# Pieces of q, k and V as closed stretches in memory, and extra rows of a strided V loaded sixteen at a time

## The chip, the cores and the metric

The kernel runs on one core of a Trainium2 chip. The metric is the device time of one execution in microseconds (us); lower is better. Arranging the inputs on the host, before they are copied to the device, is outside it.

## The reference, cut to what matters

Attention over 4 batches and 8 heads of 576 positions with 64 numbers each, then a soft mixture of 8 experts, then a two-layer network with ELU. The first four heads look at the last 32 positions, the other four at every 32nd position ("strided").

```python
B, H, S, D = 4, 8, 576, 64
scores = q @ k^T / sqrt(D)                      # per batch and head
mask_local = (rel >= 0) & (rel < 32)            # heads 0 to 3
mask_strided = (rel >= 0) & (pos_k % 32 == pos_q % 32)   # heads 4 to 7
attn = softmax(where(mask, scores, -1e9)) @ v
x = attn as (2304, 512)
# soft mixture of experts: 8 experts with 4 slots each
logits = x @ phi
slot_in = softmax(logits over tokens).T @ x
slot_out[e] = relu(slot_in[e] @ w1[e]) @ w2[e]  # w1 (8,512,1024), w2 (8,1024,512)
y = softmax(logits over slots) @ slot_out
out = elu(y @ w_in) @ w_out                     # w_in (512,2048), w_out (2048,512)
```

## The kernel before

Heads go in four pairs: p = 0, 1 are the local ones, p = 2, 3 the strided ones. For each pair q, k and V lie in SBUF on all 128 partitions; q and k have QW = 2304 numbers per partition, a strided V has WB = 4096. The host function `_lay` (line 1382) brings the inputs into that order: an array of 128 rows (72 for a strided V) for each pair, whose rows are as long as the whole partition.

The loads are taken in pieces, since attention works through 20 units in a fixed order (`ORDER`, line 39) and the first need only the first columns. `load_q` (line 224) takes columns a to b of 128 rows. `load_k` (line 227) makes two loads, of the even and of the odd rows, each into every second partition. `load_v` (line 234) takes 128 rows for a local V. For a strided V it makes two loads: 64 rows into the even partitions (line 238), and 8 more rows, for the positions from 16 on of a block of 18, into partitions 1, 17, 33, ... 113 (line 239). A strided V has odd partitions that are cleared beforehand: `lv` and line 334 do that on ACT and GpSimd, and the load waits for it. There are four such pairs of loads (two head pairs with two halves of 2048 columns), so a row of such a load is 8 KB. Every one of these loads takes, of each row of its array in memory, only a part: between two rows lie the columns of the other pieces.

All loads are issued by SP's queue, in one order. It comes from `list_order` (line 87), a list scheduler that is run as the program is made, with costs and due times written out by hand; `load_node` (line 457) gives a load's cost by its columns. After the inputs of attention come the experts' matrices, 2 MB each (`load_w`, line 358, issued at line 363), whole or in halves and smaller pieces (`LO`, `HI`), into buffers that attention's tiles leave; such an issue waits for the last reader of the buffer. `emit_w1` (line 919) multiplies the slots with the first matrices, `emit_w2` (line 1009) with the second ones, expert by expert; the matrix of the last expert comes in five pieces (line 967). `warm` (line 308) puts filler matmuls between, at line 313. After the last expert the two-layer network runs (from line 1083), with its own list of operations; its weights are loaded behind the experts' on the same queue (`load_w64`, line 971).

Of the kernel before, what the change touches and what calls it, by code (L numbers as in the profile page):

```python
# [18 lines left out]
@with_exitstack  # L19
def attn_moe_mlp(ctx, tc, q, k, v_l, v_s, phi, w1, w2, w_in, w_out, out):  # L20
    nc = tc.nc
    B, S, D = 4, q.shape[2] // 4, 64
    NT, DM = out.shape
    NE = w1.shape[0]
    w_in, w_out = w_in.bitcast(I32), w_out.bitcast(I32)
# [51 lines left out]
    QW, WB = S * B, 4096  # L77
# [127 lines left out]
    qk_t, v_t = {}, {}  # L205
# [10 lines left out]
    VT = {2: v2_sb, 3: v3_sb, 0: v0_sb[:, 0:QW], 1: v0_sb[:, QW:2 * QW]}  # L216
    for p, q_sb in ((2, q2_sb), (3, q3_sb[:, 0:QW]), (0, q3_sb[:, QW:2 * QW]), (1, q2_sb)):
# [3 lines left out]
        else:  # L221
            v_t[p] = VT[p][:, 0:WB].rearrange("p (t h w r d) -> p t h w r d", t=2, h=2, w=2, d=D)

    def load_q(p, a, b):
        nc.sync.dma_start(out=qk_t[p][0][:, a:b], in_=q[p, :, a:b])

    def load_k(p, a, b, es=((0, "S"), (1, "S"))):
        for e, eng in es:
            x = a % (QW // 2)
            (nc.sync if eng == "S" else nc.scalar).dma_start(  # L230
                out=qk_t[p][1][e:128:2, a // (QW // 2), e, x:x + b - a], in_=k[p, e:128:2, a:b]
            )

    def load_v(p, a, b):
        if p < 2:
            nc.sync.dma_start(out=VT[p][:, a:b], in_=v_l[p, :, a:b])
        else:
            nc.sync.dma_start(out=VT[p][0:128:2, a:b], in_=v_s[p - 2, 0:64, a:b])
            nc.sync.dma_start(out=VT[p][1:128:16, a:b], in_=v_s[p - 2, 64:72, a:b])

    units, cnt_p = [], {0: 0, 1: 0, 2: 0, 3: 0}
    for x in ORDER:
        p = {"L": 0, "S": 2}[x]
# [12 lines left out]
    with tc.manual_schedule():  # L256
        kz = [t.rearrange("p (h e x) -> p h e x", h=2, e=2) for t in kAB]
        A0, Q1, HW_ = 768, 1536, QW // 2
        nc.vector.memset(kz[0][:, 0, 0, 0:A0], 0.0)
        nc.gpsimd.memset(kz[0][:, 0, 1, 0:A0], 0.0)  # L260
        load_q(0, 0, Q1)
        load_k(0, 0, A0, ((1, "S"), (0, "S")))
        load_q(2, 0, HW_)
        make_identity(nc, ident)
        wm2 = misc.tile([128, 1], F32, name="wm2")
# [9 lines left out]
        for b in range(B):  # L275
            lm = lcur[32 * b:32 * b + 32]
            nc.gpsimd.affine_select(
                out=lm, in_=lm, compare_op=ALU.is_ge, fill=0.0, base=0, pattern=[[-1, 32]], channel_multiplier=1,
# [4 lines left out]
            out=lkeep[:, 0], in0=lkeep[:, 1], scalar1=0.0, scalar2=None, op0=ALU.is_equal  # L283
# [8 lines left out]
        for b in range(B):  # L292
# [3 lines left out]
                out=sm_, in_=sm_, compare_op=ALU.is_ge, fill=0.0, base=0, pattern=[[-1, MR]], channel_multiplier=1,  # L296
# [20 lines left out]
        for i, h, e, x in ((1, 0, 1, 0), (0, 0, 0, A0), (0, 0, 1, A0), (0, 1, 0, 0), (0, 1, 1, 0)):  # L317
            nc.scalar.activation(
                out=kz[i][:, h, e, x:HW_], in_=zero.to_broadcast([128, HW_ - x]), func=AF.Copy,
            )  # L320
            if i:
                load_k(2, 0, HW_, ((0, "S"), (1, "S")))
# [74 lines left out]
        def emit_ex(t):  # L397
            dT = late_at[t]
            nc.scalar.activation(
                out=dT, in_=logits[:, 192 * t:192 * t + 192], func=AF.Exp, bias=nm[:, t:t + 1],  # L400
                accum_out=dsum[:, t:t + 1],
            )
            dl[t] = dT

        def emit_dt(t):
            dT = dl[t]
            dl[t] = late_at[3 + t].rearrange("p (i x) -> p i x", x=32)
            nc.vector.transpose(out=dl[t], in_=dT.rearrange("p (i x) -> p i x", x=32))
# [19 lines left out]
        def an(eng, dur, deps, key, fn, alloc=None, instr=0):  # L428
            anodes.append((eng, dur, list(deps), key, fn, alloc, 0.0))
            if instr:  # L430
                count[len(anodes) - 1] = instr
            return len(anodes) - 1
# [24 lines left out]
        def load_node(kind, p, a, b, after=(), pre=None):  # L457
            f = {"q": load_q, "k": load_k, "v": load_v}[kind]
            if pre is not None:
                f = lambda *a: None  # L460
            need = min(users(p, kind, a, b))
            key = T[need] - (14 if kind != "v" else 9)
            dur = 128 * 4 * (b - a) / 1e6 * RATE
            if kind == "v" and p >= 2:
                dur *= 0.63
                after = [("n", y) for (k_, x), y in lv.items() if k_ == p and a <= x < b]
            post.append((key if pre is None else pre, dur, after, lambda: f(p, a, b), (kind, p, a, b)))
# [9 lines left out]
        for p in (2, 3):  # L477
            for x in range(2):
                h = (HW_ * x, HW_ * x + HW_)
# [6 lines left out]
        for x in range(2):  # L486
            h = (HW_ * x, HW_ * x + HW_)
# [334 lines left out]
        for n, (p, t, h) in enumerate(units):  # L822
            make_loads()
            evs[n] = unit_nodes(n)
            if n == max(of[3]):
                rm = an("V", 0.2, lt[4:5] + [y for m in of[2] + of[3] for y in qk[m]], T[n] + 30, lambda: nc.vector.tensor_scalar(
                    out=rmask, in0=e0, scalar1=-1.0, scalar2=-NEG, op0=ALU.add, op1=ALU.mult
# [11 lines left out]
            out=nm3[:, 0:1], in_=logits[:, 0:192], axis=AX.X))  # L839
        m = an("V", 1.3, [m], KT + 1, lambda: emit_m(0))  # L840
        x = an("A", 0.4, [m], KT + 2, lambda: emit_ex(0))
        x = an("V", 0.33, [x], KT + 2.5, lambda: emit_dt(0))
# [6 lines left out]
        x = an("P", 1.6, [x] + xe[0], KT + 3, f_acc0, ("t", r_acc), 24)  # L849

        def f_acc0e():
# [6 lines left out]
            out=nm3[:, 1:2], in_=logits[:, 192:384], axis=AX.X))  # L858
        m = an("P", 0.5, [m, rm], KT + 3.5, lambda: emit_mm(1, False), None, 4)
        m = an("V", 0.2, [m], KT + 4, lambda: emit_nm(1))  # L860
        x = an("A", 0.4, [m], KT + 4.3, lambda: emit_ex(1))
        x = an("V", 0.33, [x], KT + 4.8, lambda: emit_dt(1))
        an("V", 0.3, [lg_last[2]], KT + 4.9, lambda: nc.vector.reduce_max(
            out=nm3[:, 2:3], in_=logits[:, 384:576], axis=AX.X))
# [3 lines left out]
        for t, n in order:  # L868
# [17 lines left out]
            out=acc_sb[0], in0=acc1, scalar=wt[:, 1:2], in1=acc_sb[0], op0=ALU.mult, op1=ALU.add  # L886
# [14 lines left out]
        for x in (slice(0, 256), slice(256, 512)):  # L901
            nc.vector.scalar_tensor_tensor(
                out=acc_sb[1][:, x], in0=acc2[:, x], scalar=wt[:, 2:3], in1=acc_sb[0][:, x], op0=ALU.mult, op1=ALU.add
# [11 lines left out]
        for t in (misc.tile([128, 1024], F32, tag="pst", name="h1T"), small("xt", 768, "h1T_b", 1), ssf[:, 0:256]):  # L915
            nc.gpsimd.memset(t, 0.0)
            t = t.rearrange("p (e c s) -> p e c s", c=8, s=NS)
# [188 lines left out]
        def node(eng, dur, deps, key, fn, alloc=None, at=0.0):  # L1106
            kd, hold = HOLD.get(len(nodes), (0.0, -9.0))
            nodes.append((eng, dur, list(deps), key + kd, fn, alloc, max(at, hold)))
            return len(nodes) - 1
# [226 lines left out]
        for si, gi, s, f0, f1, y, T, parts in ev_n:  # L1336
            k = part_n[si, gi, s]
# [18 lines left out]
            x = node("V" if f0 else "A", 0.6 if f0 else 0.48, deps, key, f_ev, ("ob", rel) if f1 == NF else None)  # L1356
            o_rel[k].append(x)
            last[j] = x
            if f1 == NF:
                rel.append(node("S", 0.73, [x], key, lambda j=j, ob=ob, parts=parts: [nc.sync.dma_start(  # L1360
                    out=out[128 * j:128 * j + 128, x], in_=ob["t"][:, x]
# [20 lines left out]
def _lay(np, q, k, v, moe_phi, **rest):  # L1382
    B, H, S, D = q.shape
    def lay(x):


        l = x[:, 0:4].reshape(B, 2, 2, S // 32, 32, D).transpose(1, 5, 2, 3, 0, 4).reshape(2, 2 * D, B * S)
        s = x[:, 4:8].reshape(B, 2, 2, S // 32, 2, 2, 4, 2, D).transpose(1, 8, 7, 4, 5, 2, 6, 0, 3).reshape(2, 2 * D, B * S)
        return np.concatenate([l, s])

    vl = v[:, 0:4].reshape(B, 2, 2, S // 32, 32, D).transpose(1, 0, 4, 3, 2, 5).reshape(2, 128, 4 * S)

    vs = v[:, 4:8].reshape(B, 2, 2, S // 32, 2, 2, 8, D).transpose(1, 0, 3, 4, 5, 2, 6, 7).reshape(2, B, S // 32, 64 * D)
    vs = np.concatenate([x.reshape(2, -1, 64 * D) for x in (vs[:, :, 0:16], vs[:, :, 16:])], axis=1)
    phi = moe_phi.reshape(4, 128, -1).transpose(1, 0, 2).reshape(128, -1)

    w1, w2 = ((w.reshape(w.shape[0], -1, 128, w.shape[2]).transpose(0, 2, 1, 3).reshape(w.shape[0], 128, -1))
              for w in (rest["moe_w1"], rest["moe_w2"]))
    return dict(rest, q=lay(q), k=lay(k), v_l=vl, v_s=vs, moe_phi=phi, moe_w1=w1, moe_w2=w2)


# [23 lines left out]
```

## Time and profile before

| | us |
|---|---|
| median of 3 runs | 358.25 |
| lowest and highest | 357.84, 360.31 |
| span of the profiled execution, first to last instruction | 356.7 |
| PE busy in it | 338.3 |
| DVE, ACT, GpSimd busy in it | 261.0, 248.8, 57.4 |
| bytes moved by transfers | 69.71 MB, 195 GB/s over the span |

The profiled execution is one run with the hardware profiler on; its times are counted from the first instruction, and its span leaves out what a run has around the first and the last instruction. The rows that matter follow in a section of their own. An engine named with a q (SPq) is its queue of issues. "DMA" on the slices is the mean busy share of the 16 DMA engines.

### The profile page before, as it was taken

To read this page: it belongs to the slowest core of one execution; us is meant where nothing else is said; L and a number is where in the kernel's file an instruction comes from. 1 tells how busy PE (TensorE), PEld (TensorE's weight loads), DVE (VectorE), ACT (ScalarE), POOL (GpSimd) and SP (SyncE) were. 2 spreads that over 40 slices of the span, in tenths; PEclk is the share of its full clock that TensorE was granted. 3 is DMA by queue.
4 is the path that set the end of the run, shared out by engine and by line. 5 is a ranking of instruction groups with operands and counts; after the bars stand their busy time and mean duration, and the time that the engine had idled before them with its cause. 6 is when DMAs were issued, how large, how long until landed. Compare 5 with 4: busy or idle time off the path is not lost.

```text
span 356.7 us, 6955 instructions
## 1 busy us (share of the span) xinstructions
PE 338.3 (95%) x2678; PEld 250.5 (70%) x2678; DVE 261.0 (73%) x574; ACT 248.8 (70%) x488; POOL 57.4 (16%) x106
## 2 busy tenths in 40 slices
PE   5689889999999899999999999999999999999995
PEld 3568776783333257787888788888878888888884
DVE  5999888744605069999999999997755674576741
ACT  9488999983216079999978877767656666666650
POOL 8788534520214000000000000000000000000000
PEclk9899999999999999999999999999999999999998
DMA  7999999999999998650006041000000030032301
GB/s 266 377 378 391 407 416 424 420 410 422 423 428 419 405 403 341 243 228 2 1 0 237 1 153 82 2 0 0 2 0 1 2 119 0 31 118 88 118 2 59
DMA packets 15200, 69.71 MB, mean 195 GB/s; under 512 B 1568, under 2 KB 2080, under 8 KB 12320
## 3 DMA queue, kind: packets, MB, share of 16 engines
q1 hardware_dynamic: 15168, 69.28, 49.2%
q8 instruction: 21, 0.34, 0.4%
q14 instruction: 11, 0.09, 0.1%
HBM read 64.55 MB, written 4.72 MB: 194 GB/s over the span
## 4 chain that ended last, share of the span: by engine, by line
PE 74%; DVE 8%; DMA 8%; ACT 5%; POOL 2%; issue 2%; DVEq 0%; SPq 0%; POOLq 0%; ACTq 0%
PE ops L1312 18%; PE ops L1314 18%; PE ops L1313 18%; DMA q<-in_moe_w_dram 6%; PE hps L1264 5%; PE s_ps L923 3%; ACT bd L657 3%; PE o_ps L670 2%; DVE sc L589 1%; DMA kA<-in_k_dram 1%; PE mps L1153 1%; PE xtps L786 1%; DVE sm L613 1%; POOL bd L659 1%; DVE mx L597 1%
## 5 line engine op out<-in xcount | busy, mean ns | idle before, releaser
L1274 DVE SCALAR_TENSOR_TENSOR g<-hps,g 128x512 f32<-128x512 f32 (+1 forms) x80 | 50.6, 633 | 17.8 <-ACT g L1271 17.1
L1268 ACT ACTIVATE g<-hps 128x512 f32<-128x512 f32 (+1 forms) x80 | 44.8, 559 | 13.6 <-PE hps L1264 12.2
L1271 ACT ACTIVATE g<-g 128x512 f32<-128x512 f32 (+1 forms) x80 | 47.6, 595 | 1.5
L1280 ACT ACTIVATE ghi<-g 128x512 fp32r<-128x512 f32 (+1 forms) x40 | 23.7, 592 | 18.3 <-DVE g L1274 16.5
L1314 PE MATMUL ops<-w,glo 128*128 128x512 f32 (+1 forms) x93 | 36.0, 387 | 0.0
L1280 ACT ACTIVATE rings<-g 128x512 fp32r<-128x512 f32 (+1 forms) x39 | 23.6, 605 | 17.2 <-DVE g L1274 16.4
L1312 PE MATMUL ops<-wh,rings 128*128 128x512 f32 x80 | 31.6, 395 | 0.0
L1312 PE MATMUL ops<-w,ghi 128*128 128x512 f32 (+1 forms) x81 | 31.3, 387 | 0.0
L1313 PE MATMUL ops<-w,ghi 128*128 128x512 f32 (+1 forms) x81 | 31.3, 387 | 0.0
L1313 PE MATMUL ops<-wl,rings 128*128 128x512 f32 x80 | 31.2, 390 | 0.0
L1314 PE MATMUL ops<-wh,glo 128*128 128x512 f32 x80 | 31.2, 390 | 0.0
L1264 PE MATMUL hps<-pers 128*128 128x512 f32 (+1 forms) x80 | 30.2, 380 | 0.0
L657 ACT ACTIVATE bd<-tr 32x288 f32<-32x288 f32 (+1 forms) x60 | 28.7, 479 | 1.3
L1313 PE MATMUL ops<-w,rings 128*128 128x512 f32 x64 | 25.0, 390 | 0.0
L1312 PE MATMUL ops<-w,rings 128*128 128x512 f32 x64 | 25.0, 390 | 0.0
L1314 PE MATMUL ops<-wh,rings 128*128 128x512 f32 x62 | 24.3, 392 | 0.0
L1312 PE MATMUL ops<-wh,ghi 128*128 128x512 f32 x62 | 24.2, 390 | 0.0
L1313 PE MATMUL ops<-wl,ghi 128*128 128x512 f32 x62 | 24.2, 390 | 0.0
L1314 PE MATMUL ops<-w,rings 128*128 128x512 f32 x52 | 20.2, 389 | 0.0
L1284 DVE TENSOR_TENSOR glo<-g,ghi 128x512 fp32r<-128x512 f32 (+1 forms) x24 | 15.2, 632 | 6.8 <-ACT ghi L1280 4.5
L1314 PEld LDWEIGHTS ops<-w,glo 128*128 128x128 f32 x93 | 17.5, 188 | 3.6
L1284 DVE TENSOR_TENSOR glo<-g,rings 128x512 fp32r<-128x512 f32 (+1 forms) x24 | 15.1, 630 | 5.6 <-ACT rings L1280 4.9
(230 smaller groups left out, 763.2 us busy)
## 6 DMA issues: line engine op xcount, KB each, us to landing
v<-in_moe_w_dram SPq DMA_DIRECT2D x3, 2048.0 KB, 14.3
w<-in_moe_w_in_dram SPq DMA_DIRECT2D x3, 2048.0 KB, 11.1
out_dram<-ob SPq DMA_DIRECT2D x17, 256.0 KB, 2.0
w<-in_moe_w_dram SPq DMA_DIRECT2D x2, 2048.0 KB, 11.9
xw<-in_moe_w_dram SPq DMA_DIRECT2D x4, 1024.0 KB, 11.4
xw<-in_moe_w_out_dram SPq DMA_DIRECT2D x2, 2048.0 KB, 7.8
q<-in_q_dram SPq DMA_DIRECT2D x6, 576.0 KB, 7.7
kB<-in_k_dram SPq DMA_DIRECT2D x8, 288.0 KB, 7.3
```

Of the source, the lines that this page charges most:

```text
L657: nc.scalar.activation(out=o, in_=i, func=AF.Copy)
L670: nc.tensor.matmul(o[64 * e:64 * e + 64, j, :], v_t[p][:, max(i - 1 + k, 0), e, :], pt[:, 4 * j + 2 * e + k], start=(k == 0), stop=(k == 1),)
L923: nc.tensor.matmul(hp[32 * g:32 * g + 32, :], siT[:, POS[c], :], w_at(2 * a + g // 2, 0, 2 * c + g % 2), start=(c == CO[0]), stop=(c == CO ...
L1264: nc.tensor.matmul(t["ps"], M4[:, 128 * f:128 * f + 128], cTf[:, t0:t0 + n], start=True, stop=True)
L1268: nc.scalar.activation(out=t["g"], in_=t["ps"], func=AF.Exp)
L1271: nc.scalar.activation(out=t["g"], in_=t["g"], func=AF.Relu, scale=-1.0, bias=1.0)
L1274: nc.vector.scalar_tensor_tensor(out=t["g"], in0=t["ps"], scalar=0.0, in1=t["g"], op0=ALU.max, op1=ALU.subtract)
L1280: nc.scalar.activation(out=t["hi"], in_=t["g"], func=AF.Copy)
L1284: nc.vector.tensor_tensor(out=t["lo"], in0=t["g"], in1=t["hi"].bitcast(F32), op=ALU.subtract)
L1312: nc.tensor.matmul(o[:, x], t["hi"][:, c], hi[:, x], start=(f == f0), stop=False)
L1313: nc.tensor.matmul(o[:, x], t["hi"][:, c], lo[:, x], start=False, stop=False)
L1314: nc.tensor.matmul(o[:, x], t["lo"][:, c], hi[:, x], start=False, stop=(f == f1 - 1 and x.stop == 512))
```

## The change

The host cuts each of the arrays of q, k and V into the pieces in which they are loaded and lays them one behind the other, each as a closed stretch: rows of a piece follow each other without a gap. On the device the arrays are one-dimensional, and the new function `piece` gives a load its stretch by offset and row length. k is cut by even and odd rows too. The number, order, length and destination of the loads stay, but for line 239: the 8 extra rows of a strided V become 16, a row of zeros behind each row, and go into partitions 1, 9, 17, ... 121.

```diff
--- before.py
+++ after.py
@@ -19,7 +19,8 @@
 @with_exitstack
 def attn_moe_mlp(ctx, tc, q, k, v_l, v_s, phi, w1, w2, w_in, w_out, out):
     nc = tc.nc
-    B, S, D = 4, q.shape[2] // 4, 64
+    B, D = 4, 64
+    S = q.shape[0] // (4 * 128 * B)
     NT, DM = out.shape
     NE = w1.shape[0]
     w_in, w_out = w_in.bitcast(I32), w_out.bitcast(I32)
@@ -221,22 +222,25 @@
         else:
             v_t[p] = VT[p][:, 0:WB].rearrange("p (t h w r d) -> p t h w r d", t=2, h=2, w=2, d=D)
 
+    def piece(t, n, o, a, b):
+        return t[o + n * a:o + n * b].rearrange("(r x) -> r x", x=b - a)
+
     def load_q(p, a, b):
-        nc.sync.dma_start(out=qk_t[p][0][:, a:b], in_=q[p, :, a:b])
+        nc.sync.dma_start(out=qk_t[p][0][:, a:b], in_=piece(q, 128, p * 128 * QW, a, b))
 
     def load_k(p, a, b, es=((0, "S"), (1, "S"))):
         for e, eng in es:
             x = a % (QW // 2)
             (nc.sync if eng == "S" else nc.scalar).dma_start(
-                out=qk_t[p][1][e:128:2, a // (QW // 2), e, x:x + b - a], in_=k[p, e:128:2, a:b]
+                out=qk_t[p][1][e:128:2, a // (QW // 2), e, x:x + b - a], in_=piece(k, 64, (2 * p + e) * 64 * QW, a, b)
             )
 
     def load_v(p, a, b):
         if p < 2:
-            nc.sync.dma_start(out=VT[p][:, a:b], in_=v_l[p, :, a:b])
+            nc.sync.dma_start(out=VT[p][:, a:b], in_=piece(v_l, 128, p * 128 * QW, a, b))
         else:
-            nc.sync.dma_start(out=VT[p][0:128:2, a:b], in_=v_s[p - 2, 0:64, a:b])
-            nc.sync.dma_start(out=VT[p][1:128:16, a:b], in_=v_s[p - 2, 64:72, a:b])
+            nc.sync.dma_start(out=VT[p][0:128:2, a:b], in_=piece(v_s, 64, (p - 2) * 80 * WB, a, b))
+            nc.sync.dma_start(out=VT[p][1:128:8, a:b], in_=piece(v_s, 16, (p - 2) * 80 * WB + 64 * WB, a, b))
 
     units, cnt_p = [], {0: 0, 1: 0, 2: 0, 3: 0}
     for x in ORDER:
@@ -1391,12 +1395,23 @@
     vl = v[:, 0:4].reshape(B, 2, 2, S // 32, 32, D).transpose(1, 0, 4, 3, 2, 5).reshape(2, 128, 4 * S)
 
     vs = v[:, 4:8].reshape(B, 2, 2, S // 32, 2, 2, 8, D).transpose(1, 0, 3, 4, 5, 2, 6, 7).reshape(2, B, S // 32, 64 * D)
-    vs = np.concatenate([x.reshape(2, -1, 64 * D) for x in (vs[:, :, 0:16], vs[:, :, 16:])], axis=1)
+    x = np.stack([vs[:, :, 16:], np.zeros_like(vs[:, :, 16:])], axis=3)
+    vs = np.concatenate([x.reshape(2, -1, 64 * D) for x in (vs[:, :, 0:16], x)], axis=1)
     phi = moe_phi.reshape(4, 128, -1).transpose(1, 0, 2).reshape(128, -1)
 
     w1, w2 = ((w.reshape(w.shape[0], -1, 128, w.shape[2]).transpose(0, 2, 1, 3).reshape(w.shape[0], 128, -1))
               for w in (rest["moe_w1"], rest["moe_w2"]))
-    return dict(rest, q=lay(q), k=lay(k), v_l=vl, v_s=vs, moe_phi=phi, moe_w1=w1, moe_w2=w2)
+    def pieces(x, n, at):
+        return [x[..., a:b].reshape(-1) for a, b in zip((0,) + at, at + (n,))]
+
+    n, h = B * S, B * S // 2
+    q, k = lay(q), lay(k)
+    q = np.concatenate([y for p in range(4) for y in pieces(q[p], n, (1536 if p == 0 else h,))])
+    k = np.concatenate([y for p in range(4) for e in range(2) for y in pieces(k[p, e::2], n, (768, h) if p == 0 else (h,))])
+    vl = np.concatenate([y for p in range(2) for y in pieces(vl[p], n, (768 if p == 0 else h,))])
+    w = 32 * D
+    vs = np.concatenate([y for p in range(2) for x in (vs[p, :64], vs[p, 64:]) for y in pieces(x, 64 * D, (w,))])
+    return dict(rest, q=q, k=k, v_l=vl, v_s=vs, moe_phi=phi, moe_w1=w1, moe_w2=w2)
 
 
 def kernel(**inputs):
```

## Rows read from the trace of the kernel before

**Rows 1.** The page: span, busy tenths in 40 equal slices, DMA packets.
```profile
span 356.7 us, 6955 instructions
...
PE   5689889999999899999999999999999999999995
...
DMA  7999999999999998650006041000000030032301
...
DMA packets 15200, 69.71 MB, mean 195 GB/s; under 512 B 1568, under 2 KB 2080, under 8 KB 12320
```

**Rows 2.** Chain that ended last, in order of time: start, length (us), what.
```profile
2.16 4.82 DMA kA<-in_k_dram
...
101.89 22.21 DMA q<-in_moe_w_dram
124.10 0.04 issue
124.14 2.37 PE o_ps L1012 x8
```

**Rows 3.** Line 363, all issues of expert matrices: from issue to landing.
```profile
DMA to landing us min/median/max: 9.9/14.1/22.2
```

**Rows 4.** Timeline of PE, 96 to 132 us: start, length, engine, line, operation.
```profile
115.49 1.90 PE L1012 MATMUL o_ps<-v,h1T_b 128*32 128x512 f32 x16
117.32 1.26 PE L313 MATMUL wps<-ident 128*128 128x256 bf16 x10
...
121.28 1.05 PE L313 MATMUL wps<-ident 128*128 128x256 bf16 x8
```

**Rows 5.** Windows: engines' busy time; at the end PE's clock, DMA share, GB/s.
```profile
2.00:42.00 40.00, 32.05 (x618) 26.67 (x618) 36.07 (x110) 32.48 (x65) 33.04 (x65) 0.96 1.01 377
10.00:13.00 3.00, 1.44 (x32) 1.17 (x32) 2.93 (x12) 0.98 (x3) 2.48 (x4) 1.00 1.06 424
13.00:15.00 2.00, 1.64 (x33) 1.67 (x37) 1.97 (x7) 0.00 (x0) 0.87 (x1) 0.61 0.98 279
18.00:20.75 2.75, 2.72 (x64) 2.48 (x64) 2.71 (x9) 2.69 (x7) 2.75 (x5) 1.00 1.06 428
20.75:23.00 2.25, 2.06 (x44) 1.88 (x40) 2.22 (x7) 1.61 (x5) 1.77 (x3) 1.00 1.00 308
23.00:25.50 2.50, 1.16 (x25) 0.78 (x25) 2.46 (x10) 1.97 (x5) 1.90 (x4) 1.00 1.04 417
25.50:28.00 2.50, 2.50 (x58) 2.06 (x56) 2.47 (x10) 2.15 (x5) 2.21 (x4) 1.00 0.99 316
28.00:34.50 6.50, 6.01 (x141) 5.57 (x138) 6.33 (x21) 5.42 (x14) 6.00 (x16) 1.00 1.03 414
34.50:37.25 2.75, 2.56 (x44) 1.90 (x43) 2.27 (x8) 2.68 (x7) 1.80 (x5) 1.00 1.02 330
```

**Rows 6.** Timeline of SP's issues, line 238: start, length.
```profile
9.27 0.47 SPq L238 DMA_DIRECT2D v<-in_v_s_dram  x1
...
14.36 0.55 SPq L238 DMA_DIRECT2D v<-in_v_s_dram  x1
...
19.76 0.47 SPq L238 DMA_DIRECT2D v<-in_v_s_dram  x1
...
29.17 0.54 SPq L238 DMA_DIRECT2D v<-in_v_s_dram  x1
```

**Rows 7.** DMA issues of the strided V: KB each, median us to landing.
```profile
v<-in_v_s_dram SPq DMA_DIRECT2D x4, 512.0 KB, 8.7
...
v<-in_v_s_dram SPq DMA_DIRECT2D x4, 64.0 KB
```

**Rows 8.** Windows with halves of expert matrices alone (91 to 95), whole ones (102 to 108).
```profile
91.00:95.00 4.00, 4.00 (x41) 1.17 (x37) 3.05 (x6) 1.28 (x2) 0.84 (x2) 1.00 1.02 420
102.00:108.00 6.00, 6.00 (x57) 2.00 (x60) 0.58 (x4) 0.83 (x2) 2.02 (x4) 1.00 1.02 431
```

**Rows 9.** Lines 238 and 239: issues, duration in ns (min/median/max), first and last start.
```profile
L238 SPq DMA_DIRECT2D v<-in_v_s_dram x4: 472/506/546, 9.3 to 29.2; - x4
...
L239 SPq DMA_DIRECT2D v<-in_v_s_dram x4: 598/604/686, 10.0 to 29.8; - x4
```

## The prediction

> **What bounds the kernel now.** I read the page first. PE is busy in nearly every slice and the 16 DMA engines are busy without a gap from the first slices to about 126 us, then hardly at all [rows 1]. So the run has two parts: up to 126 us either engines or transfers can set the pace, and after it the chain is nearly all PE.
>
> The chain of waits, in order of time, decides between the two. Its DMA pieces are one at the head (line 230's second load of `kA`, which releases the first matmul) and one of 22.21 us from 101.89 us: a piece of the last expert's second matrix, landing at 124.10; PE's last `emit_w2` matmuls start 0.04 us later [rows 2]. That matrix is 2 MB in five pieces, and its piece takes 22 us only because it stands behind others: the quickest of all expert loads needs 9.9 us from issue to landing [rows 3], while 1 MB at 424 GB/s moves in 2.5 us. All these issues are on one queue. So the moment at which PE can finish the experts is the sum of all bytes ahead in the queue over the rate at which they move, from about 2 us on. Whatever makes the loads of q, k and V shorter or longer early in the run arrives at 124 us, as long as the queue never runs dry. It does not run dry for shifts of 2 or 3 us, since every expert load is issued 9.9 us or more ahead of its landing and is 5 us long at most (2 MB at 424 GB/s).
>
> How much of a gain can be cashed in? PE's order of time near the end [rows 4]: expert 5's 16 matmuls take 1.90 us and end at 117.39. What follows (matmuls of the last two experts and fillers) ends at 126.51, where the 2.37 us piece of [rows 2] ends. Without waits it would need 1.26 (filler) + 1.90 (expert 6) + 1.05 (filler) + 1.90 (expert 7) = 6.1 us against the 9.1 it takes. So at most **3.0 us** of an earlier landing can be used; beyond that PE's own chain from 90 us on is the bound.
>
> Last, the windows of the loading stage show where the queue is slow [rows 5]. Between 10 and 34.5 us it moves 414 to 428 GB/s in four stretches, and in four others, of 2.00 to 2.75 us, only 279, 308, 316 and 330. SP's issues say what stands there: four pairs of loads of the strided V, 64 rows (line 238) [rows 6] and 8 rows (line 239), which follow each. The 64 rows land 8.7 us after their issue [rows 7]; with issues at 14.36, 19.76 and 29.17 that is 23.1, 28.5 and 37.9, the ends of the last three slow stretches (23.00, 28.00, 37.25). The first pair (9.27, a shorter queue) belongs to the first.
>
> **The change, part by part.**
>
> *Closed stretches.* Every load has the same rows of the same lengths into the same partitions as before; only the distance between rows in memory shrinks (q 9,216 to 4,608 bytes, k's every second row 18,432 to 4,608, strided V 16,384 to 8,192). Does distance cost anything now? The trace has the comparison twice. Halves of expert matrices (8 KB taken from rows of 16 KB) move at 420 GB/s, whole matrices, closed in memory, at 431 [rows 8]; and 18.00 to 20.75 us, which moves only spaced rows of k, q and V, is at 428 [rows 5]. I take 0 for this part. Its bounds: no loss (closed rows move at 431), and a gain up to what the four slow stretches hide, should spacing be their cause.
>
> *The four slow stretches.* Against the 424 GB/s just ahead of them they lose 2.00 x (1 - 279/424) = 0.68, 2.25 x (1 - 308/424) = 0.62, 2.50 x (1 - 316/424) = 0.64 and 2.75 x (1 - 330/424) = 0.61, together **2.55 us**. The 64-row load of a pair cannot be the cause: most of such a load lies inside fast stretches (the 512 KB of the second pair take 1.2 us at 424 and lie mostly ahead of 20.75). What is left is the 8-row load, or its meeting with the load behind it: eight rows of 8 KB, into every 16th partition, on no more than eight of the 16 engines. The change makes it 16 rows into every 8th. It is still a short load to few partitions, now of 128 KB. Bounds: the stretches vanish (-2.55) or lose twice as much, as the bytes of these loads double (+2.55). No row separates "few engines" from "few partitions". I take 0, by the nearest row, the same pair as it runs now.
>
> [...]
>
> *Eight rows of zeros.* 4 x 64 KB more. A row is 8 KB on one engine, which moves 424/16 = 26.5 GB/s: 0.31 us, four times 1.24 us, on engines that carry no such row now. If the engine that finishes last already carries one, this is hidden (0); if not, it is 1.24. No row names engines; I take the middle, **0.62**. That is also the 256 KB over 424 GB/s.
>
> *Issue.* The 8-row issue takes 604 ns, the 64-row one 506 [rows 9]; 16 rows may cost as the latter, 0.1 us less, four times. It is covered by a queue 8.7 us long [rows 7]; without that cover 0.4 us less. The layout is made on the host, outside the timed execution.
>
> *Head.* The first matmul waits for `kA` until 6.98 [rows 2]. A shift of some tenths here moves the engines' chain and is covered by the 3.0 us of slack ahead of 126 us.
>
> **Sum.** The profiled execution has a span of 356.7 us [rows 1]; the median of the runs is 358.25, so 1.55 us lie around the span if it was an ordinary run. 0 + 0 + 0.62 + 0 gives a span of 357.3 and a time of **358.9 us**.
>
> **The rivals.**
>
> *A, forecast: the slow stretches stay.* 358.25 to 359.5 (zeros 0 to 1.24), 358.9. For: the load stays short and narrow. That the change does nothing to the time (zeros hidden too) is its lower end. 45%.
>
> *B: the slow stretches go,* because all 16 engines now carry a row each, or because V's rows are closed. 358.25 - 2.55 + (0 to 1.24) = 355.7 to 356.9, middle 356.3; below the 3.0 us that PE can use, so it arrives in full. For: the stretches begin with exactly this load. Against: twice the rows. 35%. It includes that the spacing was the cause: the fast stretches at 428 speak against that.
>
> *C: the slow stretches double.* 16 writers to few partitions slow everybody for twice as long: +2.55 + 1.24 gives 362.0. It decides from a loss of 1.2 us in each stretch on, where the time is 361.9. 9%.
>
> *D: all loads of q, k and V speed up.* From 2 to 42 us the queue moves 377 GB/s on average [rows 5]; at 428 these 40 us would take 35.2, 4.8 less, of which PE lets 3.0 through: 355.2. Past that only a different state of the engines would help. 6%; 5% is for the rest, such as PE or the first loads standing otherwise.
>
> **How the numbers follow.** Time 358.9; A's own range 358.2 to 359.5. The range for 8 in 10 reaches over most of B and part of the way to C: 356.0 to 361.0. One per cent, about what a measurement of this kernel can tell from no change, is 3.6 us: below 354.7 nothing of A to C lies, only a part of D and of the rest: faster 5%. Above 361.8 lies most of C: slower 8%. Within: 87%.
>
> **What would show it.** The 64.0 KB issue of [rows 7] becomes 128.0 KB, the bytes grow by 0.26 MB and the packets [rows 1] by 32 and what belongs to them. For A: four stretches of about 2 to 3 us near 280 to 330 GB/s again, and the last expert load landing at 124 to 125.4. For B: 410 GB/s and more from 10 to 42 us without a break, landing near 122, and PE's wait ahead of its last matmuls shorter by as much. For C: stretches of 200 to 280 GB/s or longer ones, landing after 127. I am wrong in the mechanism if the loads speed up and the end does not move (then PE or a matrix whose buffer comes free late took over), or if the end moves with no change in the landing at 124 us.

## The result and the profile after

The changed kernel takes 361.21 us (median of 6 runs, 360.49 to 361.43) against 358.34 us (6 runs, 357.84 to 360.31) before: ratio 1.0072 with an interval of 1.0059 to 1.0086, so **2.9 us slower** by the medians (2.6 by the ratio, 2.1 to 3.1), where 0.6 us was forecast: within 1%, as expected, but 0.2 us above the range. The profiled execution of after is its fastest run (360.49), with a span 2.1 us longer than before's; some 0.8 us of the median's loss is therefore not in the profile that follows.

The page of after: span and packets.
```profile
span 358.8 us, 6955 instructions
...
DMA packets 15264, 69.97 MB, mean 195 GB/s; under 512 B 1600, under 2 KB 2112, under 8 KB 12352
```
64 packets and 0.26 MB more than in [rows 1]; the instructions are the same in number. The extra rows' issue now reads 128 KB (the DMA issues, KB each and median us to landing):
```profile
v<-in_v_s_dram SPq DMA_DIRECT2D x4, 128.0 KB, 8.6
```
That line's issues, in ns (min, median, max), and the landing time of the expert loads, now line 367:
```profile
L243 SPq DMA_DIRECT2D v<-in_v_s_dram x4: 519/528/592, 10.6 to 31.0; - x4
...
DMA to landing us min/median/max: 9.7/14.5/23.1
```
The issue is shorter than [rows 9], and the queue ahead of the expert loads about as long as in [rows 3] (the longest wait 23.1 us against 22.2).

The chain that ended last, in order of time (start, length, what):
```profile
2.16 5.55 DMA kA<-in_k_dram
...
102.98 23.14 DMA q<-in_moe_w_dram
126.12 0.04 issue
126.16 2.36 PE o_ps L1016 x8
```
It has the same two long DMA pieces as the chain of [rows 2]. The first `kA` lands 0.73 us later (7.71 against 6.98), and the last expert load at 126.12 instead of 124.10: 2.02 of the span's 2.1 us are there. PE waits ahead of expert 5 already (timeline of PE; in [rows 4] these matmuls stood at 115.49 without a wait):
```profile
117.39 1.92 PE L1016 MATMUL o_ps<-v,h1T_b 128*32 128x512 f32 x16 [0.63 <-DMA v<-in_moe_w_dram]
```

The windows of the loading stage, those of [rows 5] and one more (window and its length in us; busy us of PE, PEld, DVE, ACT, POOL; at the end PE's clock, DMA share, GB/s):
```profile
2.00:42.00 40.00, 31.40 (x597) 26.34 (x597) 34.59 (x108) 31.57 (x64) 32.26 (x62) 0.96 1.01 364
13.00:15.00 2.00, 1.07 (x40) 1.07 (x44) 1.95 (x8) 0.00 (x0) 0.15 (x2) 1.00 1.02 320
18.00:20.75 2.75, 2.38 (x27) 2.17 (x25) 2.55 (x9) 2.67 (x7) 2.66 (x5) 0.50 1.06 424
20.75:23.00 2.25, 2.25 (x54) 1.97 (x54) 1.77 (x8) 2.01 (x6) 1.50 (x3) 0.92 1.02 312
23.00:25.50 2.50, 1.85 (x42) 1.70 (x40) 2.50 (x8) 1.33 (x4) 2.33 (x3) 1.00 1.02 387
25.50:28.00 2.50, 2.50 (x50) 1.87 (x52) 2.43 (x11) 2.10 (x5) 1.79 (x2) 1.00 1.05 321
28.00:34.50 6.50, 6.05 (x138) 5.40 (x140) 6.33 (x21) 5.64 (x13) 5.93 (x15) 1.00 1.01 389
34.50:37.25 2.75, 2.75 (x54) 2.19 (x56) 2.68 (x8) 2.52 (x6) 1.91 (x4) 1.00 1.04 351
37.25:42.00 4.75, 4.49 (x109) 3.94 (x104) 4.15 (x12) 4.56 (x11) 3.52 (x6) 1.00 1.04 371
```
The four slow stretches are there, at 312 to 351 GB/s, and they run over into the windows behind them: 23.00 to 25.50 falls from 417 to 387, 28.00 to 34.50 from 414 to 389, 37.25 to 42.00 to 371. In before the last one is
```profile
37.25:42.00 4.75, 4.51 (x112) 3.82 (x107) 4.51 (x12) 4.57 (x10) 3.48 (x7) 1.00 1.06 429
```
The account closes within 0.2 us: (377 - 364) GB/s over 40 us is 0.52 MB not yet moved at 42 us, and 0.26 MB more are to move; 0.78 MB at 424 GB/s is **1.84 us**, and the landing is 2.02 us late. From 42 us on little more is lost. So the loss arises while q, k and V are loaded. Two edits were made there, and the runs that follow separate them.

### The profile page after: what moved, and what is told of

It is laid out like the page before. It is cut to its first block, busy times and chain, and to the rows that moved or that the text cites. A ratio compares the mean times of both kernels' runs of the same rounds, so it can differ in the third digit from the quotient of the medians.

```text
span 358.8 us, 6955 instructions
## 1 busy us (share of the span) xinstructions
PE 338.4 (94%) x2678; PEld 250.7 (70%) x2678; DVE 260.6 (73%) x574; ACT 249.1 (69%) x488; POOL 57.6 (16%) x106
## 4 chain that ended last, share of the span: by engine, by line
PE 74%; DMA 8%; ACT 7%; DVE 5%; POOL 2%; issue 2%; DVEq 0%; SPq 0%; POOLq 0%
PE ops L1316 18%; PE ops L1318 18%; PE ops L1317 18%; DMA q<-in_moe_w_dram 6%; PE hps L1268 5%; ACT bd L661 4%; PE s_ps L927 3%; PE o_ps L674 2%; ACT xw L700 2%; DMA kA<-in_k_dram 2%; PE mps L1157 1%; PE xtps L790 1%; DVE sc L593 1%; PE s_ps L546 1%; PE wps L1377 1%
## 5 line engine op out<-in xcount | busy, mean ns | idle before, releaser
L674 PE MATMUL o_ps<-bd,v 128*64 128x128 f32 x288 | 19.2, 287 | 0.7 <-ACT bd L661 0.4
```

Source lines behind the costliest of these rows:

```text
L674: nc.tensor.matmul(o[64 * e:64 * e + 64, j, :], v_t[p][:, max(i - 1 + k, 0), e, :], pt[:, 4 * j + 2 * e + k], start=(k == 0), stop=(k == 1),)
```

## The experiments

Every run is compared with the kernel before on the same chip; its median was 358.42 us (29 runs) for the first four, 358.34 (35 runs) for the next four, 358.24 (21 runs) for the last three. Ratios stand with their 95% intervals. Of each edit the lines on the device are shown, cut to what differs; the host lays out the inputs to suit.

**The two halves of the change, each alone.** Closed layout with 8 rows (e1; the edit is shown against after):
```
-  nc.sync.dma_start(out=VT[p][1:128:8, a:b], in_=piece(v_s, 16, (p - 2) * 80 * WB + 64 * WB, a, b))
+  nc.sync.dma_start(out=VT[p][1:128:16, a:b], in_=piece(v_s, 8, (p - 2) * 72 * WB + 64 * WB, a, b))
```


> Only the closed stretches of the change: the extra rows of the strided V stay 8, into every 16th partition. Theory 1 (the 16 rows cost the time, the layout nothing): as the kernel before, 358.3 us within 0.5, ratio 0.999 to 1.001. Theory 2 (the layout costs it: in the profile after, the first load of k that the first matmul waits for landed 0.7 us later, and the slowest engine was 0.6 us late before any extra row had moved): 359 us or more, ratio above 1.0015.

and the layout of before with 16 rows, 8 of them zeros (e2; this diff and those that follow are against before, but for e9's):
```
-  out=VT[p][1:128:16, a:b], in_=v_s[p - 2, 64:72, a:b]
+  out=VT[p][1:128:8,  a:b], in_=v_s[p - 2, 64:80, a:b]
```


> Only the other part of the change: 16 rows, every second one zeros, into every 8th partition, with the layout in memory as before. Theory 1: all of the loss, 360.7 to 361.3 us, ratio 1.0065 to 1.0085. Theory 2: only the 0.6 us that 4 x 64 KB cost at 424 GB/s, 358.9 us, ratio 1.002.

e1: 359.14 us, ratio 1.0026 (1.0013 to 1.0039). e2: 360.19 us, ratio 1.0049 (1.0033 to 1.0065). 0.26% and 0.49% make 0.75%, and the whole change cost 0.72%: the halves add, some 0.9 us for the layout (0.5 to 1.4) and 1.8 us for the 16 rows (1.2 to 2.3). e1 came out as its second theory had it; e2 lies between its two. Windows of e2:
```profile
2.00:42.00 40.00, 32.29 (x632) 27.07 (x632) 35.84 (x110) 32.75 (x66) 33.08 (x65) 0.91 1.01 366
20.75:23.00 2.25, 2.22 (x51) 1.81 (x44) 2.21 (x7) 1.54 (x4) 2.25 (x4) 1.00 1.01 293
23.00:25.50 2.50, 1.81 (x37) 1.28 (x33) 2.46 (x10) 2.37 (x5) 1.91 (x3) 1.00 1.01 379
28.00:34.50 6.50, 5.71 (x133) 5.27 (x127) 6.29 (x20) 5.44 (x13) 6.07 (x15) 1.00 1.02 390
37.25:42.00 4.75, 4.64 (x119) 3.98 (x115) 4.19 (x11) 4.55 (x10) 3.42 (x7) 1.00 1.04 383
```
The overrun of the slow stretches, seen in after, is here too, with the layout of before: it belongs to the 16 rows. (377 - 366) x 40 us = 0.44 MB and the 0.26 MB of zeros make 0.70 MB, 1.65 us; the zeros as mere bytes are 0.62 of it. In e1 the windows behind the stretches lose less (390, 403 and 415 against 417, 414 and 429 before), and what is slow is the head. Windows of e1, then of before (after has 351 there):
```profile
2.00:13.00 11.00, 7.67 (x92) 6.02 (x92) 7.09 (x21) 8.97 (x14) 9.70 (x24) 1.00 0.97 349
```
```profile
2.00:13.00 11.00, 6.97 (x92) 5.17 (x92) 8.18 (x25) 8.97 (x14) 9.69 (x24) 1.00 0.98 368
```

**What makes a stretch slow: few engines, or which partitions?** Eight rows into partitions 1 to 29, every 4th, in place of every 16th (e3).
```
-  out=VT[p][1:128:16, a:b], in_=v_s[p - 2, 64:72, a:b]
+  out=VT[p][1:33:4,   a:b], in_=v_s[p - 2, 64:72, a:b]
```


> The kernel before, but its 8 extra rows go into partitions 1, 5, 9 ... 29 instead of 1, 17, 33 ... 113, so the strided heads miss those positions (a part of the result is left out). Same rows, bytes and number of engines; only the partitions written differ. Theory A (the slow stretches come from which partitions the short load writes, by the engine that writes them): they vanish, 410 to 430 GB/s from 10 to 42 us, and the time falls by 2 to 2.6 us to about 355.7 to 356.3. Theory B (they come from a load on only eight engines): nothing changes, 358.3 us and four stretches near 280 to 330 GB/s.

The stretches are gone, with the same eight rows (windows of e3):
```profile
2.00:42.00 40.00, 31.99 (x634) 27.08 (x636) 36.10 (x111) 32.79 (x66) 33.74 (x65) 0.91 1.01 398
20.75:23.00 2.25, 1.71 (x40) 1.56 (x34) 2.21 (x8) 1.15 (x4) 1.77 (x3) 1.00 1.01 406
25.50:28.00 2.50, 2.50 (x68) 2.06 (x67) 2.47 (x10) 2.19 (x5) 2.15 (x5) 1.00 1.01 410
34.50:37.25 2.75, 2.46 (x42) 2.13 (x40) 2.26 (x7) 2.66 (x7) 1.86 (x4) 1.00 1.01 404
```
Only the first, 13 to 15 us, keeps some of it (351, where e4, below, without these loads, has 391). So it is not the small number of rows. But the time fell by 0.8 us, not by the 2 to 2.6 that Theory A had; that is taken up with e4. Then the same rows, four partitions further on (e5):
```
-  out=VT[p][1:128:16, a:b], in_=v_s[p - 2, 64:72, a:b]
+  out=VT[p][5:37:4,   a:b], in_=v_s[p - 2, 64:72, a:b]
```


> As the run with 8 rows into partitions 1, 5 ... 29, but into 5, 9 ... 33: the same distance and number, shifted by four partitions (the strided heads miss their last two positions, a part of the result is left out). [...] Theory A2 (it is slow when a row goes to partitions that another of the 16 engines writes at that time, so that the order of rows over engines matters): slow stretches of 2 to 3 us near 300 to 350 GB/s again, last expert load near 123 to 124 us, time 357.7 to 358.6. [...]

They come back (windows of e5), and the time is before's again: 358.27 us, ratio 0.9999 (0.9987 to 1.0011).
```profile
20.75:23.00 2.25, 1.94 (x40) 1.62 (x36) 2.25 (x7) 1.43 (x5) 2.25 (x4) 1.00 1.02 333
25.50:28.00 2.50, 2.50 (x69) 2.06 (x69) 2.47 (x10) 2.25 (x6) 2.15 (x4) 1.00 1.00 324
34.50:37.25 2.75, 2.51 (x44) 2.20 (x42) 2.22 (x8) 2.67 (x7) 1.86 (x5) 1.00 1.00 337
```
A shift by four partitions changes neither the number of rows nor their spread, and seven of the eight partitions are the same (33 takes the place of 1; e6, below, writes both and is not slow). What it changes is which row goes to which partition. Theory A2 forecast the slow stretches and the time (357.7 to 358.6), but its cause, rows that go to partitions which another engine writes, was the author's assumption: no trace names the engine that moves a row. With the 64-row loads alone there is no slow stretch (e4, below: 422 and 411 GB/s in the first two of these windows), and the next run has none. So the runs show that for eight rows the places decide, and the rule behind it stays open.

**32 rows** into every 4th partition, 24 of them zeros: four times before's bytes (e6).
```
-  out=VT[p][1:128:16, a:b], in_=v_s[p - 2, 64:72, a:b]
+  out=VT[p][1:128:4,  a:b], in_=v_s[p - 2, 64:96, a:b]
```


> The kernel before, but with 32 extra rows instead of 8, into every 4th partition, three of four rows zeros (no part of the result is left out). Four times the bytes of these loads: 4 x 192 KB more, 1.85 us at 424 GB/s, or 1.24 us on an engine that carries two rows of 8 KB instead of one. If the slow stretches come from partitions and 32 rows go to the engines as 64 or 128 do, they vanish: 410 to 430 GB/s from 15 to 42 us and, with 2.55 us less for the stretches, 356.9 to 358.3 us in spite of more bytes. If every load under 64 rows makes them: four slow stretches, 360.5 us or more.

```profile
2.00:42.00 40.00, 32.53 (x622) 27.53 (x624) 35.62 (x110) 32.35 (x65) 32.67 (x64) 0.96 1.01 406
20.75:23.00 2.25, 2.25 (x52) 1.91 (x50) 1.77 (x6) 1.19 (x3) 1.38 (x2) 0.90 0.99 401
25.50:28.00 2.50, 2.50 (x56) 1.89 (x50) 2.43 (x10) 2.13 (x6) 2.21 (x4) 1.00 0.99 398
34.50:37.25 2.75, 2.47 (x46) 1.80 (x44) 2.26 (x8) 2.68 (x6) 1.80 (x5) 1.00 1.01 412
```
No slow stretch, although 0.79 MB more are loaded: 358.13 us, ratio 0.9997 (0.9985 to 1.0009). The lost rate had cost as much as all those zeros. Against e2's 1.0049 it shows that 16 rows are the worse choice, and not for their bytes; e6 differs from e2 in the number of rows and in their places at once, so it doesn't say which of the two it is.

**What is a stretch worth at the end?** The extra rows' loads left out (e4):
```
-  nc.sync.dma_start(out=VT[p][1:128:16, a:b], in_=v_s[p - 2, 64:72, a:b])
```

> The kernel before without the four loads of extra rows of the strided V: those positions are left out of the result. It shows all that these four short loads cost. If the slow stretches are theirs: 2.55 us for the stretches, of which up to 3.0 us in all can be used by PE: 355.3 to 355.8 us, and no stretch below 400 GB/s between 10 and 42 us. If the 64-row loads make the stretches: they stay, and the time falls by the rows' own 0.3 to 1.2 us only, to 357.1 to 358.0.

Windows of e4 and its packets:
```profile
20.75:23.00 2.25, 1.96 (x40) 1.81 (x40) 2.22 (x7) 1.52 (x4) 1.78 (x3) 1.00 1.05 422
25.50:28.00 2.50, 2.50 (x58) 2.06 (x59) 2.47 (x11) 2.14 (x6) 2.21 (x4) 1.00 1.01 411
34.50:37.25 2.75, 2.46 (x42) 1.87 (x42) 2.29 (x7) 2.68 (x6) 1.80 (x5) 1.00 1.01 386
...
DMA packets 15136, 69.45 MB, mean 195 GB/s; under 512 B 1536, under 2 KB 2048, under 8 KB 12288
```
Without these loads the stretches are gone, so they are theirs; three windows stay a little under the 400 that was expected (391, 386, and 396 from 28.00 to 34.50). But the time misses the 355.3 to 355.8 that was expected by some 2 us.

e4: 357.55 us, ratio 0.9969 (0.9947 to 0.9991). e3: 357.65 us, ratio 0.9983 (0.9968 to 0.9999). In e3 the queue is ahead by (398 - 377) x 40 us = 0.84 MB, 1.98 us, at 42 us, and the last expert load's matmuls start 1.90 us earlier than in [rows 2]; but the span is only 0.9 us shorter (355.8) and the median 0.8. Where the other microsecond went stands mostly behind that landing. The chain of e3 that ended last:
```profile
115.93 11.22 DMA xw<-in_moe_w_out_dram
127.14 0.02 issue
127.17 0.04 ACT xw L991
127.21 0.53 issue
127.74 0.27 ACT mp L1160
```
and its timelines of PE and ACT:
```profile
122.24 2.41 PE L1012 MATMUL o_ps<-q,ss 128*32 128x512 f32 x8 [0.23 <-DMA q<-in_moe_w_dram]
...
128.06 0.71 PE L1174 MATMUL mps<-mp,e 128*128 128x128 f32 x4 [0.84 <-ACT mp L1160]
...
125.92 0.68 ACT L991 ACTIVATE xw<-xw 128x512 f32<-128x512 f32 x1 [0.52 <-DMA xw<-in_moe_w_out_dram]
127.17 0.67 ACT L991 ACTIVATE xw<-xw 128x512 f32<-128x512 f32 x1 [0.57 <-DMA xw<-in_moe_w_out_dram]
```
against the same operations before (timelines of ACT and PE, kernel before):
```profile
127.29 1.44 ACT L991 ACTIVATE xw<-xw 128x512 f32<-128x512 f32 x2
...
128.98 0.71 PE L1174 MATMUL mps<-mp,e 128*128 128x128 f32 x4
```
Line 991 decodes pieces of `w_out`, the next matrix in the queue. Before, ACT does two of them back to back. In e3 the work ahead of them is 1.9 us earlier, but the second piece has only landed at 127.14, ACT waits for each of the two, and PE's line 1174 gains 0.92 us instead of 1.9. e4's chain has the same load in it (12.38 us long, to 126.58). So in both a gain at the expert loads is cut to about half by the `w_out` load behind them. The queue's lead had shrunk before that, too (windows of before, then of e3):
```profile
66.00:70.00 4.00, 3.94 (x54) 2.76 (x52) 2.95 (x11) 3.89 (x10) 3.47 (x5) 1.00 1.00 426
```
```profile
66.00:70.00 4.00, 3.94 (x56) 2.76 (x52) 2.53 (x11) 3.86 (x10) 3.51 (x5) 1.00 0.96 377
```
With 411 and 398 GB/s in the 4 us that follow, 0.25 MB of the lead of 0.84 MB are lost there. SP's line 363 issues its next load at 65.10 us, only 0.42 us earlier than before's 65.52, after a wait of 12.9 us for PE's line 683 (11.7 before). That fits a queue that is 2 us ahead and runs short of work, since PE frees the buffers only 0.4 us sooner.

**Where does the layout cost?** V closed alone (e7: of the change only the edits of `load_v`) and q and k closed alone (e8: only those of `load_q` and `load_k`), both with 8 rows:

> Closed stretches for both kinds of V alone, 8 extra rows as before, q and k as before. Where the layout's cost comes from the first loads (q and k): 6 to 10 us at 353 to 365 GB/s as in all kernels with spaced rows, and the time of the kernel before, 358.4 within 0.4. Where closed rows are slower in general: about half of the 0.9 us that all closed loads together cost, 358.8 us or more.

> Closed stretches for q and k alone, V and its 8 extra rows as before. Where the layout's cost comes from the first loads: 6 to 10 us at 334 to 342 GB/s as in the two kernels with all loads closed (354 to 365 in the four with spaced rows), and all of the 0.9 us: 359.0 to 359.5, ratio 1.0015 to 1.003. Otherwise 358.4 to 358.8.

e7: 358.52 us, ratio 1.0014 (1.0001 to 1.0026). e8: 358.79 us, ratio 1.0017 (1.0003 to 1.0032). The intervals overlap, so the times don't divide the loss, and e7's lies above 1 as well: closed V may have a share. Nor does the window that the expectations named: from 6 to 10 us e7 has 349 GB/s and e8 365, both against what was expected. The wider one from 2.00 to 13.00, chosen only then, has 370 in e7, near the 368 of before, and 339 in e8:
```profile
2.00:13.00 11.00, 7.11 (x92) 5.28 (x92) 6.81 (x20) 8.69 (x14) 9.40 (x24) 1.00 0.95 339
```
So q and k were divided: pairs 1 to 3 closed (e10), and pair 0, which holds the run's first loads, closed alone (e11). The lines that are added on the host:
```
e10, q (k alike):
+  q = np.concatenate([q[0].reshape(-1)] + [y for p in range(1, 4) for y in pieces(q[p], n, (h,))])
e11, q (k alike):
+  q = np.concatenate(pieces(q[0], n, (1536,)) + [q[1:].reshape(-1)])
```


> Closed rows for q and k of pairs 1 to 3 alone; pair 0, whose pieces are the first loads of the run, lies as before; V and its 8 rows too. Theory 1 (the layout costs at the first loads of pair 0, with rows of 1.5 and 3 KB): 2 to 13 us at 363 GB/s or more, last expert load starts PE near 124.1, time 358.3, ratio 1.000. Theory 2 (it costs at every load of q and k): 2 to 13 us at 339 to 355 GB/s, near 125, time 358.8, ratio 1.0015.

> The reverse: closed rows for q and k of pair 0 alone. Theory 1: 2 to 13 us at 339 to 351 GB/s, time 358.8, ratio 1.0015. Theory 2: 2 to 13 us at 355 GB/s or more, time 358.4 to 358.5, ratio 1.0005.

e10: 358.32 us, ratio **0.9997** (0.9987 to 1.0007). e11: 359.21 us, ratio **1.0030** (1.0018 to 1.0042). q and k of the later pairs may lie as they like; pair 0's closed pieces cost 1.1 us (0.6 to 1.5). The window of e10, then of e11, from 2 to 13 us, and e11's first piece of the chain (4.82 us long in [rows 2]):
```profile
2.00:13.00 11.00, 7.13 (x100) 5.46 (x103) 8.48 (x27) 8.97 (x14) 9.69 (x24) 0.98 0.98 375
```
```profile
2.00:13.00 11.00, 7.70 (x92) 6.01 (x92) 7.34 (x22) 8.97 (x14) 9.83 (x24) 1.00 0.98 359
```
```profile
2.16 5.36 DMA kA<-in_k_dram
```
The five kernels with pair 0 closed (after, e1, e8, e9, e11) move 339 to 359 GB/s in this window, those with it spaced (before, e2 to e7, e10) 363 to 383. In e1, e8 and after the loss at the head is still there at 42 us (370, 369 and 364 GB/s from 2 to 42 us, against 377). In e11's trace it is not: 359 is above the 339 to 351 that Theory 1 had asked for, 2 to 42 us moves 380, and the last expert load starts PE at 124.15, as before (124.14). That profiled execution is e11's fastest run (358.45), and no trace shows how the 1.1 us of its median come about. So that pair 0 costs time is shown by the times; that it does so by way of the head is seen in the other kernels. Why the first loads start more slowly when their rows adjoin in memory is not settled: number and lengths of packets are the same, and no run varies the distance of rows by itself.

**The change with 32 rows** (e9): closed layout, and e6's partitions; against after:
```
-  VT[p][1:128:8, a:b], in_=piece(v_s, 16, (p - 2) * 80 * WB + 64 * WB, a, b)
+  VT[p][1:128:4, a:b], in_=piece(v_s, 32, (p - 2) * 96 * WB + 64 * WB, a, b)
```

> The change with 32 rows (24 of them zeros) into every 4th partition in place of its 16 into every 8th. Theory 1 (two separate costs: the closed layout some 0.9 us at the head, the 16 rows some 1.8 us through longer slow stretches): the stretches go as in e6 (380 GB/s and more in each window from 10 to 42 us), the head stays slow (2 to 13 us: 339 to 351 GB/s), the time is 358.1 + 0.9 = 359.0, ratio about 1.002. Theory 2 (the closed layout and the extra rows only hurt together): 361, ratio 1.007, stretches near 300 GB/s.

359.49 us, ratio 1.0037 (1.0024 to 1.0050). From 18 to 42 us every window has 405 GB/s and more, and from 2.00 to 13.00 the head is slow (346). So the two costs are separate: with the stretches taken away about half of the change's loss goes, and the layout's share stays. At 1.2 to 1.3 us it is above the 0.9 expected, and the interval leaves out the ratio of 1.002 that was expected. The windows from 10 to 18 us miss the 380 as well (366, 280 and 362); between 13 and 15 us the DMA share falls to 0.72, a gap in the loads that e6 does not have and that no run explains. No kernel here that does the whole work beats before: e6 is level with it, and needs more memory for it.

## Why the prediction was right or wrong

**The steps that failed.** Two terms were taken as 0 and were not: the slow stretches grew by some 1.1 us, and the closed stretches cost some 0.9 us, with bounds that allowed no loss. The chain and the queue were right. The zeros' bytes came as forecast; their 0.62 us was not measured by itself.

**The bound: right for a loss, wrong for a gain.** A delay in the queue did arrive in full: 1.84 us of it at 42 us, 2.02 us at the landing, 2.1 us in the span. But the step "How much of a gain can be cashed in?" allowed up to 3.0 us, because it asked only what PE needs behind [rows 4]. It left out that the queue has another load behind the last expert's, `w_out`, on which ACT's line 991 waits. e3 measured 1.9 us at the landing and 0.8 to 0.9 at the end. "It does not run dry for shifts of 2 or 3 us" failed for a gain, too: from 66 to 74 us e3's queue moved 0.25 MB less than before's. So rival B's 355.7 to 356.9 was not reached even where the stretches went: 357.65 in e3, 357.55 in e4, 358.13 in e6.

**The slow stretches: their owner was right, their size was not.** They belong to the extra rows' loads, they stayed when 16 rows took the place of 8, and that was the forecast. But "I take 0, by the nearest row, the same pair as it runs now" was the term that was mis-sized: together with the zeros' 0.62 us the 16 rows cost 1.8 us (e2, interval 1.2 to 2.3), so some 1.1 us of it are longer stretches. With twice the rows in such places the stretches run over into the windows behind them (e2: 379 GB/s against 417 before, 390 against 414, 383 against 429); that is about half of rival C's price (2.55 + 1.24 = 3.8 us). The sentence 'No row separates "few engines" from "few partitions".' overlooked one column of [rows 5]: in the four slow stretches the DMA share is 0.98 to 1.02, so the 16 engines were as good as always busy in them, and moved fewer bytes in that time. Idle engines were not what was lacking. The runs then spoke for the partitions: with eight rows the queue moves 404 to 410 GB/s in e3 and 324 to 337 in e5.

**Rival B's first reason fell.** It had the stretches go because all 16 engines now carry a row each. No trace names the engines of a load; what the profiles show is packets under 512 B: 1,536 without these loads (e4), 1,568 with 8 rows, 1,600 with 16 (after, e2), which is 8 and 16 for each of the four loads, and no row says what these packets are. But e2, with 16 rows, is slower than 8 rows (ratio 1.0049), and e3's eight have no stretch from 18 us on. So 16 rows in place of 8 were not what was lacking.

**Closed stretches: the term taken as 0 cost 0.9 us** (e1, interval 0.5 to 1.4), and its bounds ("no loss") shut the true value out. The argument came from rows of the middle and the end of the loading, and for q and k of the later pairs it holds (e10, ratio 0.9997). By the times the loss is in the first loads, those of pair 0 (e11, 1.0030), with a share of V not excluded (e7, 1.0001 to 1.0026). The prediction had no spaced-against-closed row from the head. Its sentence on the head, "a shift of some tenths here moves the engines' chain and is covered", looked at PE's first matmul only; in after, e1 and e8 the same slow loads also push everything behind them in the queue.

**Zeros, issue.** 0.26 MB as forecast, 64 packets where "32 and what belongs to them" was expected: the packets of 8 KB or more are 2,880 before and 2,912 after, one more for each of the 32 rows of zeros. Which engine carries such a row, and so whether the 1.24 us of the upper bound arise, no trace shows. Issue 528 ns against 604, covered.

The sum that the runs give is 0.9 (layout) + 0.62 (zeros as bytes) + 1.1 (longer stretches) = 2.6 us, for 2.6 measured by the ratio and 2.9 by the medians.

## What to carry to other kernels

A short load into a few spaced partitions can cost more than its bytes, since the whole queue runs slower while it is in flight (308 to 330 GB/s here against 414 to 428): look at the rate and the DMA share in windows around it, and try other partitions (404 to 410 in e3), or more rows at another spacing, even with zeros in them (398 to 412 in e6). A comparison of memory layouts taken in the middle of a run said nothing here about the first loads: closed rows moved at 431 GB/s against 420 in [rows 8], and from 2.00 to 13.00 us at 339 to 359 against 363 to 383. And before a gain in a queue is counted in full, look which load stands behind the one it speeds up and who waits for it (e3: 1.9 us at the landing, 0.8 to 0.9 at the end).

## What was unexpected of the hardware

- With the number of rows the same, their places decided whether the short load slowed the queue: with eight rows at partitions 1, 5, ... 29 it moves 404 to 410 GB/s in the three windows (e3), with the same eight at 5, 9, ... 33 324 to 337 (e5), though seven of the eight partitions are the same. Why is open.
- In the slow stretches the DMA engines are not idle: at 308 GB/s their share is 1.00, at 428 it is 1.06 ([rows 5]).
- 256 KB in 32 rows disturbed less (398 to 412 GB/s in the same windows, e6) than 64 KB in eight rows (308 to 330, [rows 5]).
- Rows that adjoin in memory were not faster here than rows 9 to 18 KB apart: no difference for the later loads of q and k (ratio 0.9997, e10), and a loss for the first ones (1.0030, e11).
